# Weight slices converted in two pieces of 768 elements instead of three of 512

## The chip, the cores and the metric

The kernel runs on one core of a Trainium2 chip. The metric is the device time of one launch in microseconds (us). The kernel before was timed three times: 909.64, 910.88 and 911.83 us, median 910.88 us. The execution that was profiled took 909.49 us.

## The reference

Talking-heads attention is followed by a gated feed-forward layer. All inputs are 64-bit floats; the output is 32-bit.

```
scores = scale * q @ k^T                      # 4 batches, 12 heads, 448 x 448, depth 64
scores = einsum('bhij,hg->bgij', scores, w_pre)
attn   = exp(scores - max) / (sum + 1e-9)     # softmax over j
attn   = einsum('bhij,hg->bgij', attn, w_post)
x      = (attn @ v) as 1792 tokens x 768
h      = x @ w_in                             # 768 -> 2048
out    = (h * sigmoid(1.702 h)) @ w_out       # 2048 -> 768
```

## The kernel before

Attention runs in 180 softmax steps of ten query rows by twelve heads (45 a batch). A step is: gather of 120 score rows from DRAM (`r`, L295), mixing product on TensorE (`mx`, L312), maximum on VectorE (`nm`, L322), exponential on ScalarE (`e`, L332), sum on GpSimd (`rs`, L343), reciprocal on VectorE (L348), weighting on GpSimd (`wr`, L353), second mixing product on TensorE (`pp`, L363), and a copy out by ScalarE (`p`, L419). Batches 0 and 1 work in 32 bits, batches 2 and 3 in pairs of 16-bit numbers. Score products (`qk`, L247) run ahead of the steps. Every twelve steps make a chunk, and when its last copy is done, two context products (`av`, L441) multiply it with v. They share one PSUM bank. Their results become x, which the feed-forward layer reads.

The feed-forward layer (`h`, L604, and `po`, L642) takes the weights in 16 slices: `w_in` and `w_out` in eight each. [...] So `conversion` (L500 to L583) rebuilds 32-bit floats from the two 32-bit halves and then splits them into an upper and a lower 16-bit part. A slice goes through this in NP pieces of HW = WN // NP elements. For each piece there is a fetch on SyncE's queue (`w`, L513), `magnitude` on ScalarE (L520), `least`, `shift`, `rest` and `sign` on VectorE (L524, L528, L534, L540; each reads what the one before wrote) and `size`, a sum of squares on ScalarE with a read of its accumulator (L99). Once all pieces have a size, one small product on TensorE adds them over the partitions (L111, on `w_m`), VectorE makes a scale of it, and each piece gets `w_upper` on ScalarE (L568) and `w_lower` on VectorE (L573). The slice is then stored to DRAM (L579) and read back from there for each unit of the feed-forward layer (L592). Conversions run from 28 us (first fetch) to about 407 us (last store).

The sums of squares for v (`squares`, L134, which also calls L99) have the same form: a small product L111 on `mv`, whose result VectorE turns into a scale that the context's copies need.

The order of the work is not written out by hand. Each operation is entered with `add`: engines, a duration estimate (`occ`), dependences, a due time and, for a transfer, its size in MB. A planner (`run_all`) keeps a clock per engine and a model of the DMA queue. At each turn it takes the operation that can start first, the earlier due one where several can, and emits it. All instructions are in order on their engine, so the estimates set the order everywhere, also that of instructions that have nothing to do with the weights. Buffers are planned by tag: `w64` is the 64-bit staging, `wf` the 32-bit pieces, `wc` the 16-bit result.

Of the kernel before, what the change touches and what calls it, by code (L numbers as in the profile page):

```python
# [11 lines left out]
BF16 = mybir.dt.bfloat16  # L12
# [7 lines left out]
B, H, S, D = 4, 12, 448, 64  # L20
# [19 lines left out]
def attention_then_feed_forward(ctx, tc, q, k, v, w_pre, w_post, w_in, w_out, out):  # L40
# [6 lines left out]
    keep, stat, flow = pool("keep"), pool("stat", 4), pool("flow")  # L47
# [42 lines left out]
    def square_sum(x, m, eng):  # L90

        n = 1
        for d in x.shape[1:]:
            n *= d
        waste = flow.tile([128, 512], BF16, name="waste", tag="waste" + eng)[:x.shape[0], :n]
        if len(x.shape) == 3:
            waste = waste.rearrange("p (a b) -> p a b", b=x.shape[2])
        if eng == "A":
            nc.scalar.activation(waste, x, AF.Square, accum_out=m)  # L99
        else:  # L100
            nc.vector.scalar_tensor_tensor(
                waste, x, 1.0, x, op0=ALU.mult, op1=ALU.mult, accum_out=m
            )
# [380 lines left out]
    def scale_x(b):  # L484
# [8 lines left out]

    wd = {(kind, s): dram.tile([128, 2, WN], F16, name=f"wd{kind}_{s}", tag=f"wd{kind}_{s}")
          for kind in range(2) for s in range(NS)}
    NP = 3
    HW = WN // NP
    WF = 5

    def conversion(kind, s):  # L500

# [296 lines left out]
    def gated_by(x):  # L798

        if not 0 < x <= N:  # L800
            return []
        if x not in gates:
            gates[x] = add("-", 0.0, lambda: None, expos_at(x - 1), x, 0.0)
        return [gates[x]]
# [250 lines left out]
    def conversion_tasks(kind, s, first):  # L1055

        c = conversion(kind, s)
        due, sizes, low, wfs, pair = first + 7, [], [], [], []
        for a in range(NP):
            w64, wf = [], []  # L1060
            wfs.append(wf)
            j = add("SP", 0.4, lambda a=a: c["fetch"](a), gated_by(first + 2 * a), first + 2 * a, size=0.524, takes=[("w64", w64)])
            for n, (name, occ) in enumerate((("magnitude", 0.62), ("least", 0.35), ("shift", 0.35), ("rest", 0.61), ("sign", 0.61))):
                j = add("D" if n else "A", occ, lambda a=a, name=name: c[name](a), [j], due, occ + 0.09, takes=[] if n else [("wf", wf)])
                w64.append(j)
                if n:
                    wf.append(j)
            sizes.append(add("A", 0.63, lambda a=a: c["size"](a), [j], due + 0.2, 0.73))
            wf.append(sizes[-1])
        k = sums(c["total"], c["parts"], sizes, due)  # L1070
        k = conv_scale[kind, s] = add("D", 1.0, c["scale_w"], [k], due, 1.1)
        for a in range(NP):
            u = add("A", 0.62, lambda a=a: c["w_upper"](a, "A"), [k] + low[:0] + ([ups[0]] if a else []), due + 0.5, 0.72,
                    takes=[] if a else [("wc", pair)])
            if not a:
                ups = [u]
            low.append(add("D", 0.66, lambda a=a: c["w_lower"](a), [u], due + 0.5, 0.75))
            wfs[a] += [u, low[a]]
            pair += [low[a]] + ([u] if a else [])
        j = conv_done[kind, s] = add("SP", 0.4, c["store"], low, due, size=0.786)  # L1080
        pair.append(j)
# [3 lines left out]
    for b in range(B):  # L1085
        for c in range(NCH):
# [3 lines left out]
            for pr in range(NPAIR):  # L1090
                x = base - (18 if c == NCH - 1 else 17) + 2 * pr if c else base - 11 + pr
                if b == 0 and c == 1:
                    x = pr
# [13 lines left out]
    for n in range(2 * NS):  # L1107
        x = 7 * n if n <= NS else 7 * NS + 5 * (n - NS)
# [4 lines left out]
    for i in range(N):  # L1113
        if i + AHEAD < N:
            b, g = steps[i + AHEAD]
            n = i + AHEAD
            gathers[n] = add("SP", 0.4, lambda n=n: gather(n), sends.get((b, g // GPC), []), i,
                             size=0.215, takes=[("r", r_home[n])], behind=gathers.get(n - 1))
# [42 lines left out]
    for u in range(NU):  # L1161
        s, b = units[u]
        due = due_of["h", u, 0, 0]
# [5 lines left out]
        for fc in range(SF):  # L1169
            gen, th = [], []  # L1170
            j = None
# [87 lines left out]
```

## Time and profile before

| | before |
|---|---|
| timed runs, median (lowest to highest) | 910.88 us (909.64 to 911.83) |
| profiled execution | 909.49 us |
| its span on the core | 907.8 us |
| TensorE (PE) busy in the span | 878.1 us, 97% |
| VectorE (DVE) busy | 633.6 us, 70% |
| ScalarE (ACT) busy | 630.5 us, 69% |
| GpSimd (POOL) busy | 342.8 us, 38% |

The span runs from the first to the last instruction of the program; the execution has 1.69 us around it. In a view by windows the first two numbers of a row are the stretch and its length, then come the busy times of PE, of its weight loads (PEld), DVE, ACT and POOL with instruction counts, the granted TensorE clock (1.00 is full), the share of time that the DMA engines were busy, and GB/s. Length minus PE busy is PE's idle time in the stretch. In a view in order of time, the bracket at the end tells the idle time of the engine before the row and who ended it.

### The profile page before, as it was taken

What the parts mean: (1) busy time and instruction counts of PE and PEld (TensorE: products, weight loads), DVE (VectorE), ACT (ScalarE), POOL (GpSimd) and SP (SyncE); (2) the same over time, 40 slices, a digit from 0 to 9 for tenths busy, and PEclk for the clock granted to TensorE, in tenths of its full rate; (3) what the DMA queues carried; (4) which work ended last, traced back from release to release, by engine and by line L of the source; (5) the groups of instructions that cost most, each with busy time, mean ns of one, the idle gap of its engine ahead of it and who ended that gap; (6) DMA issues with size and microseconds to landing.
All of it is one profiled execution on the core that took longest, in us unless ns stands there. A gap on an engine that the chain in (4) does not pass through costs nothing.

```text
span 907.8 us, 19395 instructions
## 1 busy us (share of the span) xinstructions
PE 878.1 (97%) x7062; PEld 538.5 (59%) x7062; DVE 633.6 (70%) x1471; ACT 630.5 (69%) x1391; POOL 342.8 (38%) x538
## 2 busy tenths in 40 slices
PE   7889999999999999999999999999999999999998
PEld 5465666666566566655666656665656666545554
DVE  3668887678789988999678876679676664342233
ACT  2778888698877877876788797676776765323442
POOL 0212222222124221566346745547254663203332
PEclk9989999999999999999999999999999999999999
DMA  7878999998997796688587486568553432243422
GB/s 237 277 285 290 304 326 319 323 308 268 336 331 251 238 300 198 219 234 311 169 265 251 147 258 175 175 180 243 163 154 127 152 97 91 109 139 121 139 74 92
DMA packets 66402, 196.85 MB, mean 217 GB/s; under 512 B 7714, under 2 KB 32546, under 8 KB 66306
## 3 DMA queue, kind: packets, MB, share of 16 engines
q1 hardware_dynamic: 66306, 195.62, 66.7%
q8 instruction: 55, 0.90, 0.4%
q14 instruction: 41, 0.34, 0.1%
HBM read 138.96 MB, written 56.62 MB: 215 GB/s over the span
## 4 chain that ended last, share of the span: by engine, by line
PE 66%; DVE 13%; DMA 7%; ACT 7%; POOL 3%; issue 2%; SPq 1%; ACTq 0%; POOLq 0%; DVEq 0%
PE h L604 19%; PE po L642 18%; PE mx L312 5%; PE pp L363 5%; PE qk L247 3%; PE av L441 3%; PE av L452 3%; DMA vb<-in_v_dram 2%; PE qk L257 2%; DMA sd<-sc 2%; DVE nm L322 2%; DMA r<-sd 2%; PE mx L315 2%; PE pp L400 1%; PE pp L402 1%
## 5 line engine op out<-in xcount | busy, mean ns | idle before, releaser
L604 PE MATMUL h<-x,wt 128*128 128x448 f16 x1152 | 246.5, 352 | 2.0 <-DVE sc L273 0.9
L642 PE MATMUL po<-g,wt 128*128 128x448 f16 x1152 | 239.0, 352 | 2.4 <-DVE th L623 2.1
L604 PEld LDWEIGHTS <-wt 128*128 128x128 f16 x1152 | 108.9, 98 | 105.6 <-issue 15.6
L642 PEld LDWEIGHTS <-wt 128*128 128x128 f16 x1152 | 110.2, 98 | 101.5 <-issue 8.0
L343 POOL TENSOR_SCALAR rs<-sm 120x1 f32<-120x1 f32 x180 | 45.2, 251 | 319.0 <-ACT e L332 311.0
L322 DVE TENSOR_REDUCE nm<-mx 120x1 f32<-120x448 f32 x180 | 111.0, 617 | 36.4 <-PE mx L317 17.9
L670 POOL TENSOR_TENSOR acc<-acc,pt 128x448 f32<-128x448 f32 x69 | 78.7, 1141 | 114.0 <-ACT pt L664 113.3
L363 PEld LDWEIGHTS pp<-wr,e 120*112 120x112 f32 x720 | 85.1, 177 | 37.5 <-issue 18.7
L387 POOL TENSOR_TENSOR a<-w,a 120x448 f16<-120x448 f32 (+1 forms) x90 | 96.0, 1066 | 22.7 <-POOL w L373 11.2
L623 DVE SCALAR_TENSOR_TENSOR th<-th,h 128x448 f32<-128x448 f32 x64 | 39.5, 618 | 92.4 <-ACT th L619 92.1
L363 PE MATMUL pp<-wr,e 120*112 120x120 f32 x720 | 90.9, 270 | 3.9 <-POOL wr L353 3.7
L312 PE MATMUL mx<-r,wa 120*120 120x448 f32 x180 | 87.1, 569 | 5.8 <-DMA r<-sd 4.4
L332 ACT ACTIVATE e<-mx,nm,c 120x448 f32<-120x448 f32 (+1 forms) x90 | 65.3, 725 | 33.2 <-DVE nm L324 23.3
L373 POOL TENSOR_SCALAR w<-e,rs 120x448 f32<-120x448 f32 (+1 forms) x90 | 64.9, 721 | 42.7 <-DVE rs L348 25.1
L666 DVE SCALAR_TENSOR_TENSOR acc<-po,ct,acc 128x448 f32<-128x448 f32 x99 | 66.8, 677 | 15.9 <-PE po L642 15.3
L332 ACT ACTIVATE e<-mx,nm 120x448 f32<-120x448 f32 (+1 forms) x90 | 56.8, 632 | 28.5 <-DVE nm L322 24.9
L664 ACT ACTIVATE pt<-po,ct 128x448 f32<-128x448 f32 x69 | 43.6, 633 | 46.6 <-PE po L642 46.6
L381 ACT ACTIVATE a<-e,rs 120x448 f16<-120x448 f32 (+1 forms) x90 | 59.8, 668 | 20.2 <-DVE rs L348 17.4
L427 DVE TENSOR_TENSOR p<-pp,p 112x480 f16<-112x480 f32 (+1 forms) x90 | 58.3, 649 | 10.8 <-ACT p L423 10.1
L619 ACT ACTIVATE th<-h,ct 128x448 f32<-128x448 f32 x64 | 40.3, 630 | 36.0 <-PE h L604 36.0
L273 DVE SCALAR_TENSOR_TENSOR sc<-qk,sc 120x448 f16<-120x448 f32 (+1 forms) x96 | 55.5, 615 | 10.5 <-ACT sc L269 9.7
L423 ACT CAST p<-pp 112x480 f16<-112x480 f32 (+1 forms) x90 | 50.2, 557 | 17.8 <-PE pp L402 17.6
(141 smaller groups left out, 1604.7 us busy)
## 6 DMA issues: line engine op xcount, KB each, us to landing
wt<-wd SPq DMA_DIRECT2D x64, 768.0 KB
r<-sd SPq DMA_DIRECT2D x176, 210.0 KB
sd<-sc SPq DMA_DIRECT2D x66, 420.0 KB
w<-in_moe_w_in_dram SPq DMA_DIRECT2D x24, 512.0 KB
w<-in_moe_w_out_dram SPq DMA_DIRECT2D x24, 512.0 KB
wd<-w_p SPq DMA_DIRECT2D x16, 768.0 KB
sd<-sc SPq DMA_DIRECT2D x24, 308.0 KB
out_dram<-acc SPq DMA_DIRECT2D x24, 224.0 KB
```

Source lines behind the costliest of these rows:

```text
L312: nc.tensor.matmul(mx[:K, :S], st["wa"][:K, :K], r[:K, :], start=True, stop=True)
L322: nc.vector.tensor_reduce(nm[:K], row["mx", i][:K, :S], axis=AX.X, op=ALU.max, negate=True)
L332: nc.scalar.activation(e[:K], row.pop(("mx", i))[:K, :S], AF.Exp, bias=row.pop(("nm", i))[:K, 0:1], scale=1.0 if b < WHOLE else st["c", b] ...
L363: nc.tensor.matmul(pp[:CP, jc * K:(jc + 1) * K], e[:K, jc * CP:(jc + 1) * CP], wr[:K, :, :n], start=True, stop=True,)
L373: nc.gpsimd.tensor_scalar(w[:K], e[:K], row["rs", i][:K, 0:1], 1.0, op0=ALU.mult, op1=ALU.mult)
L381: nc.scalar.activation(a1[:K], row["e", i][:K], AF.Copy, scale=row["rs", i][:K, 0:1])
L387: nc.gpsimd.tensor_tensor(a2[:K], row.pop(("w", i))[:K], row["a1", i][:K], op=ALU.subtract)
L427: nc.vector.tensor_tensor(p[:, 1], row.pop(("pp", i)), p[:, 0], op=ALU.subtract)
L604: nc.tensor.matmul(h, w[:, i, c, fc * 128:(fc + 1) * 128], x[:, j, c, :], start=(n == 0), stop=(n == len(terms) - 1),)
L642: nc.tensor.matmul(po, w[:, j, fc, e * 128:(e + 1) * 128], g[:, i, fc, :], start=(n == 0), stop=(n == len(terms) - 1),)
L666: nc.vector.scalar_tensor_tensor(a, po, c, a, op0=ALU.mult, op1=ALU.add)
L670: nc.gpsimd.tensor_tensor(a, a, st.pop(("pt", u, e)), op=ALU.add)
```

## The change

NP goes from 3 to 2, so a piece has 768 elements. `w64` has NP buffers as before (its size in bytes stays), `wf` has three buffers of 768 in place of five of 512, and the unused output of `square_sum` (`waste`) grows to 768 columns. The planner's estimates for the pieces are raised to suit, and so the planner also orders the rest anew. The number of products on TensorE is the same; each sum on `w_m` now has two columns.

```diff
@@ -92,7 +92,7 @@
         n = 1
         for d in x.shape[1:]:
             n *= d
-        waste = flow.tile([128, 512], BF16, name="waste", tag="waste" + eng)[:x.shape[0], :n]
+        waste = flow.tile([128, 768], BF16, name="waste", tag="waste" + eng)[:x.shape[0], :n]
         if len(x.shape) == 3:
             waste = waste.rearrange("p (a b) -> p a b", b=x.shape[2])
         if eng == "A":
@@ -493,9 +493,9 @@
 
     wd = {(kind, s): dram.tile([128, 2, WN], F16, name=f"wd{kind}_{s}", tag=f"wd{kind}_{s}")
           for kind in range(2) for s in range(NS)}
-    NP = 3
+    NP = 2
     HW = WN // NP
-    WF = 5
+    WF = 3
 
     def conversion(kind, s):
 
@@ -1059,22 +1059,22 @@
         for a in range(NP):
             w64, wf = [], []
             wfs.append(wf)
-            j = add("SP", 0.4, lambda a=a: c["fetch"](a), gated_by(first + 2 * a), first + 2 * a, size=0.524, takes=[("w64", w64)])
-            for n, (name, occ) in enumerate((("magnitude", 0.62), ("least", 0.35), ("shift", 0.35), ("rest", 0.61), ("sign", 0.61))):
+            j = add("SP", 0.4, lambda a=a: c["fetch"](a), gated_by(first + 2 * a), first + 2 * a, size=0.786, takes=[("w64", w64)])
+            for n, (name, occ) in enumerate((("magnitude", 0.83), ("least", 0.48), ("shift", 0.48), ("rest", 0.88), ("sign", 0.88))):
                 j = add("D" if n else "A", occ, lambda a=a, name=name: c[name](a), [j], due, occ + 0.09, takes=[] if n else [("wf", wf)])
                 w64.append(j)
                 if n:
                     wf.append(j)
-            sizes.append(add("A", 0.63, lambda a=a: c["size"](a), [j], due + 0.2, 0.73))
+            sizes.append(add("A", 0.85, lambda a=a: c["size"](a), [j], due + 0.2, 0.95))
             wf.append(sizes[-1])
         k = sums(c["total"], c["parts"], sizes, due)
         k = conv_scale[kind, s] = add("D", 1.0, c["scale_w"], [k], due, 1.1)
         for a in range(NP):
-            u = add("A", 0.62, lambda a=a: c["w_upper"](a, "A"), [k] + low[:0] + ([ups[0]] if a else []), due + 0.5, 0.72,
+            u = add("A", 0.84, lambda a=a: c["w_upper"](a, "A"), [k] + low[:0] + ([ups[0]] if a else []), due + 0.5, 0.94,
                     takes=[] if a else [("wc", pair)])
             if not a:
                 ups = [u]
-            low.append(add("D", 0.66, lambda a=a: c["w_lower"](a), [u], due + 0.5, 0.75))
+            low.append(add("D", 0.93, lambda a=a: c["w_lower"](a), [u], due + 0.5, 1.02))
             wfs[a] += [u, low[a]]
             pair += [low[a]] + ([u] if a else [])
         j = conv_done[kind, s] = add("SP", 0.4, c["store"], low, due, size=0.786)
```

The first place is VectorE around step 22, where the planner had put the third piece of slice w0_1 between the maximum of step 22 (`nm_22`) and its reciprocal (`rs_22`). Before:

```order
L322 TENSOR_REDUCE nm_22_1010<-mx_22_991 120x1
L524 TENSOR_SCALAR w0_1_f2_1005<-w0_1_f2_1005 128x512
L528 TENSOR_SCALAR w0_1_f2_1005<-w0_1_f2_1005 128x512
L183 TENSOR_REDUCE e_wm_88<-wall2_940 128x1
L186 TENSOR_SCALAR e_wm_88<-e_wm_88 128x1
L187 TENSOR_SCALAR e_wm_88<-e_wm_88 128x1
L191 RECIPROCAL s_wm_1036<-e_wm_88 128x1
L192 TENSOR_SCALAR s_wm_1036<-s_wm_1036 128x1
L193 TENSOR_SCALAR wm1_86<-w_mix_82,s_wm_1036 120x120
L194 SCALAR_TENSOR_TENSOR wm2_87<-w_mix_82,s_wm_1036,wm1_86 120x120
L534 SCALAR_TENSOR_TENSOR w0_1_f2_1005<-w0_1_64_2_895,w0_1_f2_1005 128x512
L348 RECIPROCAL rs_22_1044<-rs_22_1044 120x1
```

and now:

```order
L322 TENSOR_REDUCE nm_22_982<-mx_22_963 120x1
L183 TENSOR_REDUCE e_wm_88<-wall2_914 128x1
L186 TENSOR_SCALAR e_wm_88<-e_wm_88 128x1
L187 TENSOR_SCALAR e_wm_88<-e_wm_88 128x1
L191 RECIPROCAL s_wm_995<-e_wm_88 128x1
L192 TENSOR_SCALAR s_wm_995<-s_wm_995 128x1
L193 TENSOR_SCALAR wm1_86<-w_mix_82,s_wm_995 120x120
L194 SCALAR_TENSOR_TENSOR wm2_87<-w_mix_82,s_wm_995,wm1_86 120x120
L115 TENSOR_REDUCE w0_1_n_1019<-pp_20_975 128x1
L348 RECIPROCAL rs_22_1017<-rs_22_1017 120x1
```

Three conversion instructions are gone from between them; the sum for the slice (L115, on `w0_1_n`) has come in.

The second place is TensorE where chunk 3 of batch 0 ends: step 44 is its last step, and `av_0_3_0` its first context product. Before:

```order
L363 MATMUL pp_42_1843<-wr_42_1796,e_42_1779 112x120 x4
L247 MATMUL qk_1_1_2_0_1855<-kf1_1_1216,qf1_1_1221 120x448
L247 MATMUL qk_1_1_2_1_1856<-kf1_1_1216,qf1_1_1221 120x448
L363 MATMUL pp_43_1870<-wr_43_1840,e_43_1820 112x120 x4
L363 MATMUL pp_44_1887<-wr_44_1882,e_44_1859 112x96 x4
L441 MATMUL av_0_3_0_1904<-p_0_3_1624,vf0_0_367 64x88 x16
L441 MATMUL av_0_3_0_1904<-p_0_3_1624,vf1_0_412 64x88 x8
L312 MATMUL mx_45_1934<-r_45_1813,wa_206 120x448
```

and now:

```order
L312 MATMUL mx_45_1795<-r_45_1722,wa_206 120x448
L363 MATMUL pp_43_1802<-wr_43_1790,e_43_1766 112x120 x4
L247 MATMUL qk_1_1_2_0_1815<-kf1_1_1177,qf1_1_1182 120x448
L247 MATMUL qk_1_1_2_1_1816<-kf1_1_1177,qf1_1_1182 120x448
L312 MATMUL mx_46_1824<-r_46_1727,wa_206 120x448
L363 MATMUL pp_44_1836<-wr_44_1832,e_44_1798 112x96 x4
L247 MATMUL qk_1_1_3_0_1851<-kf1_1_1177,qf1_1_1182 120x448
L247 MATMUL qk_1_1_3_1_1852<-kf1_1_1177,qf1_1_1182 120x448
L312 MATMUL mx_47_1861<-r_47_1747,wa_206 120x448
L363 MATMUL pp_45_1872<-wr_45_1859,e_45_1841 112x120 x4
L441 MATMUL av_0_3_0_1880<-p_0_3_1577,vf0_0_356 64x88 x16
L441 MATMUL av_0_3_0_1880<-p_0_3_1577,vf1_0_406 64x88 x8
```

Between `pp_44` and `av_0_3_0`, which follow each other directly before, there are now four rows: two halves of a score product, `mx_47` and `pp_45`.

The third place is TensorE at the end of the first chunk, with the sum for v (L111, on `mv_0`). Before:

```order
L363 MATMUL pp_10_601<-wr_10_596,e_10_575 112x120 x4
L111 MATMUL pp_10_601<-mv_0_470,ones_77 128x6
L363 MATMUL pp_11_629<-wr_11_619,e_11_606 112x120 x4
L441 MATMUL av_0_0_0_658<-p_0_0_290,vf0_0_367 64x120 x16
L441 MATMUL av_0_0_0_658<-p_0_0_290,vf1_0_412 64x120 x8
```

and now:

```order
L363 MATMUL pp_10_588<-wr_10_585,e_10_561 112x120 x4
L363 MATMUL pp_11_604<-wr_11_598,e_11_582 112x120 x4
L111 MATMUL pp_11_604<-mv_0_454,ones_77 128x6
L441 MATMUL av_0_0_0_637<-p_0_0_290,vf0_0_356 64x120 x16
L441 MATMUL av_0_0_0_637<-p_0_0_290,vf1_0_406 64x120 x8
```

The sum for v has moved behind `pp_11`. Such moves go on in the first half of the program; behind the first context products of batch 2 (`av_2_0_0`), TensorE's order is the same as before. On SyncE's queue the first gathers and fetches keep their order: r_4, piece 0 of w0_0, r_5, piece 1, a score store, r_6.

## Rows read from the trace of the kernel before

**Rows 1.** Page, busy time of the engines (us, share, instructions).

```profile
PE 878.1 (97%) x7062; PEld 538.5 (59%) x7062; DVE 633.6 (70%) x1471; ACT 630.5 (69%) x1391; POOL 342.8 (38%) x538
```

**Rows 2.** Windows by stage, columns as told under the table above.

```profile
25.00:58.15 33.15, 28.29 (x148) 15.86 (x146) 22.91 (x60) 28.79 (x72) 6.91 (x21) 0.98 0.93 311
58.15:75.00 16.85, 14.83 (x129) 11.10 (x130) 11.03 (x27) 10.46 (x27) 1.82 (x6) 0.84 0.56 181
75.00:173.00 98.00, 93.02 (x721) 61.58 (x720) 75.88 (x190) 81.35 (x200) 25.38 (x68) 1.00 0.97 323
173.00:250.00 77.00, 77.00 (x493) 47.56 (x492) 62.02 (x162) 66.44 (x163) 16.29 (x41) 1.00 0.94 304
250.00:430.00 180.00, 174.20 (x1298) 107.44 (x1298) 166.33 (x373) 137.47 (x309) 70.07 (x104) 1.00 0.81 260
430.00:907.80 477.80, 471.38 (x4193) 282.67 (x4191) 287.15 (x640) 299.50 (x613) 220.92 (x289) 1.00 0.50 158
```

**Rows 3.** Waits of PE: line, what ended them, us in total, times, longest.

```profile
PE mx L312 <- DMA r<-sd: 4.4, 5, 2.6
PE pp L363 <- POOL wr L353: 3.7, 6, 1.4
```

**Rows 4.** Conversion lines, 512 elements each: duration ns min/median/max, first and last start.

```profile
L520 ACT ACTIVATE w_f<-w x48: 650/671/707, 32.1 to 382.2; 128x512 f32<-128x512 f32 x48
L524 DVE TENSOR_SCALAR w_f<-w_f x48: 406/419/990, 32.8 to 388.8; 128x512 f32<-128x512 f32 x48
L534 DVE SCALAR_TENSOR_TENSOR w_f<-w,w_f x48: 673/692/1622, 34.6 to 394.4; 128x512 int32<-128x512 int32 x48
L540 DVE SCALAR_TENSOR_TENSOR w_f<-w,w_f x48: 673/689/1650, 35.3 to 397.9; 128x512 int32<-128x512 int32 x48
L99 ACT ACTIVATE waste<-w_f x48: 612/630/661, 37.5 to 399.3; 128x512 bf16<-128x512 f32 x48
L99 ACT ACTIVATION_READ_ACCUMULATOR waste<-w_f x48: 185/187/223, 38.0 to 399.8; 128x1 f32 x48
L568 ACT ACTIVATE w_p<-w_f,w_s x48: 705/718/743, 48.9 to 405.2; 128x512 f16<-128x512 f32 x48
L573 DVE SCALAR_TENSOR_TENSOR w_p<-w_f,w_s,w_p x48: 732/746/1525, 49.6 to 406.4; 128x512 f16<-128x512 f32 x48
```

**Rows 5.** Nearest other sizes, same columns; L353 is the softmax weighting on POOL.

```profile
L84 DVE TENSOR_SCALAR w_n<-w_n x16: 133/146/154, 46.8 to 402.5; 128x1 f32<-128x1 f32 x16
L222 DVE SCALAR_TENSOR_TENSOR kp<-kb,s_k,kp x6: 1140/1145/1379, 277.7 to 496.1; 128x896 f16<-128x896 f32 x6
L99 ACT ACTIVATE waste<-ka x12: 562/577/593, 232.7 to 469.4; 128x448 bf16<-128x448 f32 x12
L353 POOL TENSOR_SCALAR wr<-wp,rs x90: 358/366/803, 24.1 to 355.7; 120x120 f32<-120x120 f32 x88, 96x120 f32<-96x120 f32 x2
```

**Rows 6.** PE in order of time: start, us, instruction, [idle before <-releaser].

```profile
36.65 1.01 PE L312 MATMUL mx<-r,wa 120*120 120x448 f32 x2 [1.02 <-DMA r<-sd]
55.82 0.39 PE L111 MATMUL pp<-mv,ones 112*128 112x6 f32 x2 [1.43 <-ACT waste L99]
58.15 2.07 PE L441 MATMUL av<-p,vf 112*64 112x120 f32 x18 [0.66 <-ACT p L419]
...
93.79 1.07 PE L363 MATMUL pp<-wr,e 120*112 120x120 f32 x8 [1.43 <-POOL wr L353]
...
159.58 2.04 PE L441 MATMUL av<-p,vf 112*64 112x88 f32 x48 [1.94 <-ACT p L419]
```

**Rows 7.** DVE in order of time around 92 us, same columns.

```profile
90.08 0.43 DVE L528 TENSOR_SCALAR w_f<-w_f 128x512 int32<-128x512 int32 x1
...
92.09 0.69 DVE L534 SCALAR_TENSOR_TENSOR w_f<-w,w_f 128x512 int32<-128x512 int32 x1
92.70 0.16 DVE L348 RECIPROCAL rs<-rs 120x1 f32<-120x1 f32 x1
```

**Rows 8.** Window of the second fall of the granted clock, columns as in rows 2.

```profile
56.59:63.42 6.83, 5.97 (x54) 5.31 (x52) 4.60 (x14) 3.56 (x10) 0.00 (x0) 0.50 0.90 344
```

## The prediction

> **What bounds the kernel now.** I read the page's busy times first, then windows by stage, then PE's own waits, and last the stretches in which PE waits. The page shows PE busy for 878.1 us of a span of 907.8 us [rows 1]. The change leaves PE's products as they are, so it can only work on the 29.7 us in which PE is idle, and on the clock. The windows say where these lie: 4.9 us between 25 and 58 us, 2.0 up to 75, 5.0 up to 173, none from there to 250 (the feed-forward products then fill every hole), 5.8 from 250 to 430, and 6.4 behind that [rows 2]; the rest, 5.6, is the start before the first fetch. The order of PE is the same again soon after 430 us, and the conversions are over, so I leave the last stretch and the start as they are. What can move is 4.9 + 2.0 + 5.0 + 5.8 = 17.7 us. The other engines matter only where they end one of these waits. From 250 to 430 us VectorE is the tightest of them, 166.3 of 180 us busy; ScalarE has 137.5 [rows 2].
>
> **The change part by part.** *Fewer, longer instructions.* Each of the 16 slices loses five VectorE instructions (L524, L528, L534, L540, L573), three on ScalarE (L520, L99, L568), one accumulator read and one fetch. No instruction of 768 elements is in the trace, so I bound it. If time went wholly by elements, 768 would take 1.5 times 512 and nothing were saved. The nearest wider row is L222 with 896 elements, median 1145 ns [rows 5]; against L573 with 512, 746 ns [rows 4], that is 1.04 ns an element, and 768 would take 1012 ns. I take this slope for the three-operand lines. L573 then goes from 3 x 746 = 2238 to 2 x 1012 = 2024 ns, a saving of 214; L534 from 3 x 692 to 2 x 958, 160; L540 (689) 157. L524 stands at 419 ns, and a one-element instruction of its kind at 146 [rows 4, 5], which gives 0.53 ns an element, 555 ns at 768 and a saving of 147; L528 is of the same kind, another 147. VectorE saves 0.83 us a slice, 13.2 us in all, between 0 and that. On ScalarE, L99 takes 577 ns at 448 and 630 at 512 [rows 4, 5], 0.83 ns an element, so 212 more for 768: L520 saves 247, L568 294, L99 206 and one read 187, in all 0.93 us a slice, 14.9 us. Nearly all of this lies beside PE's work; it counts only at the places below.
>
> [...]
>
> *The end of the first chunk, 54 to 58 us.* PE waits 1.43 us before the sum for v, for ScalarE's squares, and 0.66 us before the first context product, for ScalarE's copies [rows 6]. In the new order `pp_11` stands ahead of that sum, which covers some of the first wait, but the context product still waits for the same copies behind the squares. What is gained is what ScalarE has less to do up to there: slice w0_0 whole (0.93) less the longer first piece of w1_0 (0.21), 0.72 us. I take -0.7; the ends are 0 and -2.1 (both waits).
>
> *Step 22, 92 us.* PE waits 1.43 us at `pp_22` [rows 6] for `wr`, which waits for the reciprocal at 92.70. Ahead of that reciprocal VectorE ran L524, L528 and L534 of a third piece, 0.42 + 0.43 + 0.69 us [rows 4, 7], and this piece no longer exists; a sum of 0.15 us moves in. I take -1.3; the ends are 0 and -1.4. Next late is then nothing on VectorE, but `pp_23`, which has its own chain.
>
> *The end of batch 0, 158 us.* `av_0_3_0` waits 1.94 us for the copy of `pp_44` [rows 6]. In the new order a score product, `mx_47` and `pp_45` stand between them, each as long as the 1.0 us of an `mx` [rows 6], or nearly. Three such blocks cover 1.94 us. I take -1.9; the ends are 0 (if `mx_47` waits for its gather in turn) and -1.9.
>
> *The rest up to 430 us.* Six slices (18 of the 48 pieces) lie between 250 and 430 us, so VectorE has 6 x 0.83 = 5.0 us less in a stretch in which it is idle for 13.7 us and PE for 5.8 [rows 2]. If VectorE were the sole cause, PE would gain 5.0; if each wait has its own chain, nothing. I take -1.5, nearer to nothing, because the waits are short and several end at ScalarE or at a transfer.
>
> *Larger fetches.* A piece of 128 x 768 numbers of 8 bytes is 768 KB instead of 512 KB. In the first microseconds r_5 stands behind one piece and r_6 behind two. At 311 GB/s [rows 2] 256 KB more take 0.84 us, so the gathers come 0.8 and 1.7 us later. PE waits there for gathers already: the longest after the start is 1.02 us at 36.65 [rows 6], of 4.4 us in all [rows 3]. Cover is thin, since no feed-forward product exists yet. I take +0.8; the ends are 0 and +1.7. Past 45 us PE does not wait for gathers, and there are 16 fetches less on SyncE's queue, which I count as nothing.
>
> *Waits that the new order makes.* The planner deals out the first half anew; some places will have less ahead of a wait than before. I take +1.0, two waits of 0.5 us, the size of the smaller ones; the ends are 0 and +5, a doubling of one stretch's idle time (75 to 173 us).
>
> The sum is -0.7 - 1.3 - 1.9 - 1.5 + 0.8 + 1.0 = -3.6 us. The profiled execution took 909.49 us, so 905.9; the median of the runs is 1.39 us above the profiled one, so 907.3 us.
>
> *The clock.* [...] The fall follows the idle stretch at 54 to 58 us. As that gets only 0.7 us shorter, I expect the fall to stay, at 0, with ends of -3.0 (it goes) and +3.0 (a second one comes).
>
> **The rivals.** *The gaps are dealt anew, and nothing is won.* The waits on the way of a softmax step are set by a planner whose estimates differ from the chip's by tenths of a microsecond; another order has another set of about 18 us of gaps. For it: the waits are many and short, and each has another releaser. Against it: three of the largest have a named cause that the change takes away. It gives the time of before, 910.9 us.
>
> [...]
>
> *Slower: the larger pieces ahead of the first gathers.* Its place is 28 to 58 us. r_5 and r_6 come 0.8 and 1.7 us later, `pp_5` stands behind them with nothing to cover, and the softmax chain carries the delay on into the first chunk's end, where a longer idle stretch brings a second fall of the clock. Price: +1.7, +3.0 for the clock, and +1.0 of new waits, against half of the 5.4 us of gains: +3.0, 912.5 us profiled, 913.9 as a median. For it: PE's waits for gathers in this stretch and a DMA share of 0.93 [rows 2]. Against it: the first slice's data is the same in total, and later gathers stand behind no more than before. It decides once the delays exceed the gains by 1.8 us.
>
> *The conversion gets no cheaper* (768 elements take 1.5 times 512): then the terms of ScalarE and of the rest fall away, -1.3 - 1.9 + 0.8 + 1.0 = -1.4, 909.5 us, inside the first rival's band.
>
> **How the numbers follow.** A measurement of this kernel can tell about 0.2%, 1.8 us, so "same" is 909.1 to 912.7 us. The forecast has 0.53, with its own range of 903.5 to 909. The gaps dealt anew, together with a conversion that gets no cheaper, have 0.27, and the larger pieces 0.20. The range is 902.5 to 913.5: below it lies only the case in which the clock's fall goes and the long stretch gains its 5.0 as well, and above it the worst of the slower case, together some 0.15. Faster 0.53, same 0.27, slower 0.20.
>
> **What would show it.** PE idle between 75 and 173 us falls from 5.0 to about 2; the bracket of 1.94 before an `av` near 158 us and that of 1.43 near 92 us are gone. VectorE's busy time falls by about 13 us, ScalarE's by up to 15. L534 stands near 958 ns and L524 near 555. The forecast is wrong if PE's idle time between 25 and 430 us stays at 17 us or more, and the slower rival is right if waits for `r` grow before 58 us and the clock is at 0.50 for more than one stretch behind 25 us.

## The result and the profile after

The kernel after takes 916.25 us (median of four runs, 915.99 to 917.81), the kernel before 910.26 us in the same comparison (909.51 to 911.83). The ratio is 1.0067 with a 95% interval of 1.0048 to 1.0086: slower by 0.7%, where 907.3 us was predicted. The profiled execution of after took 917.81 us, with a span of 916.1 us.

The page of after, busy time of the engines, answers to [rows 1]:

```profile
PE 880.4 (96%) x7062; PEld 539.5 (59%) x7062; DVE 622.4 (68%) x1392; ACT 622.9 (68%) x1327; POOL 346.8 (38%) x533
```

VectorE has 11.2 us less to do and ScalarE 7.6 us less. The conversion's own lines fell by more, on VectorE from 150.4 to 131.7 us and on ScalarE from 104.1 to 92.0; the rest of each engine's work changed too, because the planner may give a copy or an addition to either engine and dealt those anew as well. PE has the same 7062 products but 2.3 us more busy time. The span is 8.3 us longer: 2.3 us of PE's busy time and 6.0 us of idle time (29.7 before, 35.7 after).

The durations of the conversion lines in after (ns, min/median/max) answer to [rows 4]:

```profile
L520 ACT ACTIVATE w_f<-w x32: 881/912/946, 33.9 to 388.2; 128x768 f32<-128x768 f32 x32
L524 DVE TENSOR_SCALAR w_f<-w_f x32: 537/553/881, 34.8 to 391.9; 128x768 f32<-128x768 f32 x32
L534 DVE SCALAR_TENSOR_TENSOR w_f<-w,w_f x32: 939/957/1278, 36.7 to 394.4; 128x768 int32<-128x768 int32 x32
L540 DVE SCALAR_TENSOR_TENSOR w_f<-w,w_f x32: 937/953/1794, 37.8 to 395.8; 128x768 int32<-128x768 int32 x32
L573 DVE SCALAR_TENSOR_TENSOR w_p<-w_f,w_s,w_p x32: 1000/1012/1020, 49.7 to 410.3; 128x768 f16<-128x768 f32 x32
```

The forecast had 958 for L534, 555 for L524 and 1012 for L573. The instructions are not what went wrong, and the third rival, a conversion that gets no cheaper, falls. The windows of after, columns as in [rows 2], show where the time went:

```profile
25.00:58.15 33.15, 27.82 (x125) 14.56 (x124) 17.34 (x39) 23.04 (x54) 7.06 (x18) 0.85 0.88 300
58.15:75.00 16.85, 12.89 (x126) 9.74 (x125) 11.70 (x31) 11.47 (x27) 1.10 (x4) 0.90 0.52 172
75.00:173.00 98.00, 89.66 (x615) 57.99 (x615) 71.34 (x159) 76.70 (x175) 27.70 (x66) 0.97 0.89 291
173.00:250.00 77.00, 76.59 (x562) 48.43 (x559) 57.33 (x135) 61.82 (x144) 15.82 (x41) 1.00 0.93 310
250.00:430.00 180.00, 175.51 (x1306) 109.26 (x1304) 162.11 (x354) 137.92 (x294) 68.06 (x98) 1.00 0.82 262
```

PE's idle time is the length of a row less its first busy time. From 25 to 75 us it is 9.3 us (before: 6.9), from 75 to 250 us 8.7 (5.0), from 250 to 430 us 4.5 (5.8). Only the last of these gained. Together they rose by 4.9 us; the other 1.1 us of new idle time lie before 25 and behind 430 us. Next PE's waits in after (us in total, times, longest), which answer to [rows 3]:

```profile
PE pp L363 <- POOL wr L353: 8.0, 7, 3.1
PE mx L312 <- DMA r<-sd: 4.8, 3, 2.6
```

Waits for gathers took 0.4 us more than before; the waits for `wr` went from 3.7 to 8.0 us. The longest after the start, in order of time, against [rows 6]:

```profile
31.02 1.39 PE L312 MATMUL mx<-r,wa 120*120 120x448 f32 x2 [1.84 <-DMA r<-sd]
...
39.42 0.94 PE L363 MATMUL pp<-wr,e 120*112 120x120 f32 x3 [3.08 <-POOL wr L353]
...
99.33 1.55 PE L363 MATMUL pp<-wr,e 120*112 120x120 f32 x8 [2.17 <-POOL wr L353]
...
135.00 0.38 PE L111 MATMUL pp<-w_m,ones 128*128 128x2 f32 x2 [2.25 <-ACT waste L99]
...
137.35 1.94 PE L363 MATMUL pp<-wr,e 120*112 120x120 f32 x8 [1.01 <-POOL wr L353]
```

These are `mx_4`, `pp_5`, `pp_23` (the step behind the one whose wait of 1.43 us the change took away), the sum for slice w0_2 and `pp_35`. The 1.94 us before `av_0_3_0` are gone. The wait of `mx_4` is for r_4, which stands ahead of the first piece of weights on SyncE's queue; `mx_5` and `mx_6`, whose gathers stand behind pieces, do not wait. Before, `mx_4` started at nearly the same time, and PE came there without a pause:

```profile
30.87 0.92 PE L312 MATMUL mx<-r,wa 120*120 120x448 f32 x2
```

From the start of `mx_5` to that of `pp_5` it is 5.5 us before (33.02 to 38.54) and 5.3 after (34.12 to 39.42). So the chain of that step is no longer than it was; PE has less to do beside it. Last, the stretches of after in which the granted clock is at its lower level, columns as in [rows 8]:

```profile
31.50:34.90 3.40, 3.40 (x7) 0.96 (x6) 0.89 (x3) 1.51 (x3) 0.47 (x2) 0.50 1.00 301
38.30:45.20 6.90, 5.78 (x16) 2.96 (x18) 3.63 (x6) 4.03 (x9) 1.06 (x1) 0.51 1.00 308
62.20:65.60 3.40, 3.40 (x40) 3.36 (x36) 3.30 (x5) 1.01 (x3) 0.00 (x0) 0.51 0.61 214
99.80:103.20 3.40, 3.40 (x18) 2.10 (x19) 1.67 (x4) 0.61 (x2) 0.00 (x0) 0.50 0.97 338
137.30:140.70 3.40, 3.35 (x11) 2.51 (x12) 2.35 (x3) 2.45 (x5) 0.00 (x0) 0.50 0.06 21
```

Five stretches, 20.5 us in all, against two with 10.2 us before. Each follows a wait of PE: 1.84 us at 29.2, 3.08 at 36.3, 1.94 in two pieces around 60, 2.17 at 97.2 and 2.25 at 132.8 us. Not every wait is followed by a fall: the 1.94 us before `av_0_3_0` in before were not.

### The profile page after: what moved, and what is told of

Read it like the earlier page. It is cut to its first block, busy times and chain, and to the rows that moved or that the text cites. A ratio compares the mean times of both kernels' runs of the same rounds, so it can differ in the third digit from the quotient of the medians.

```text
span 916.1 us, 19201 instructions
## 1 busy us (share of the span) xinstructions
PE 880.4 (96%) x7062; PEld 539.5 (59%) x7062; DVE 622.4 (68%) x1392; ACT 622.9 (68%) x1327; POOL 346.8 (38%) x533
## 4 chain that ended last, share of the span: by engine, by line
PE 74%; DMA 9%; DVE 8%; ACT 3%; POOL 2%; issue 2%; SPq 1%; ACTq 0%; DVEq 0%; POOLq 0%
PE po L642 20%; PE h L604 20%; PE pp L363 6%; PE mx L312 6%; PE qk L247 3%; PE av L441 3%; PE av L452 3%; PE qk L257 3%; DMA r<-sd 2%; PE mx L315 2%; PE pp L400 2%; PE pp L402 1%; PE pp L401 1%; PE mx L317 1%; PE mx L316 1%
## 5 line engine op out<-in xcount | busy, mean ns | idle before, releaser
L343 POOL TENSOR_SCALAR rs<-sm 120x1 f32<-120x1 f32 x180 | 52.8, 293 | 325.5 <-ACT e L332 320.6
L670 POOL TENSOR_TENSOR acc<-acc,pt 128x448 f32<-128x448 f32 x65 | 75.4, 1160 | 109.9 <-ACT pt L664 109.3
L363 PE MATMUL pp<-wr,e 120*112 120x120 f32 x720 | 92.8, 273 | 8.9 <-POOL wr L353 8.0
L312 PE MATMUL mx<-r,wa 120*120 120x448 f32 x180 | 89.4, 581 | 6.7 <-DMA r<-sd 4.8
L666 DVE SCALAR_TENSOR_TENSOR acc<-po,ct,acc 128x448 f32<-128x448 f32 x103 | 69.5, 677 | 16.5 <-PE po L642 16.1
L664 ACT ACTIVATE pt<-po,ct 128x448 f32<-128x448 f32 x65 | 41.2, 633 | 47.7 <-PE po L642 47.7
L353 POOL TENSOR_SCALAR wr<-wp,rs 120x120 f32<-120x120 f32 (+1 forms) x90 | 44.9, 499 | 52.7 <-DVE rs L348 43.7
```

Source lines behind the costliest of these rows:

```text
L312: nc.tensor.matmul(mx[:K, :S], st["wa"][:K, :K], r[:K, :], start=True, stop=True)
L363: nc.tensor.matmul(pp[:CP, jc * K:(jc + 1) * K], e[:K, jc * CP:(jc + 1) * CP], wr[:K, :, :n], start=True, stop=True,)
L666: nc.vector.scalar_tensor_tensor(a, po, c, a, op0=ALU.mult, op1=ALU.add)
L670: nc.gpsimd.tensor_tensor(a, a, st.pop(("pt", u, e)), op=ALU.add)
```

## Experiments

**Sizes and order taken apart.** The planner deals out the order from its estimates, so the change alters two things at once. To part them, the planner's order was written out as a list of operations with their engines and emitted as it stands. big_old and big_old02 have the order of before, small_new that of after (the list itself and the lines that name the operations are left out here):

```diff
-    run_all()
+    for text in zlib.decompress(base64.b64decode(ORDER)).decode().split():
+        key, e = text.split(":")
+        j = by_key[key]
+        j["f"](e) if len(j["eng"]) > 1 else j["f"]()
```

> Pieces of 768 as in the change, but every other instruction in the order that the kernel before has on each engine: the old order is written into the kernel as a list, each slice's two pieces take the places of the old second and third piece, and the fetches the places of the old first and second. Theory 'order' (the loss comes from the new order of the rest): 906 to 911 us, PE idle between 25 and 173 us at 12 us or less. Theory 'size' (the loss comes from longer instructions on the way of the softmax step and larger fetches ahead of the gathers): 914 to 918 us, PE idle there near 17 us.

> As the first kernel with pieces of 768 in the old order, but the two pieces take the places of the old first and third piece, so the work on a slice begins as early as before. 'Order': 906 to 912 us, if it was the later start that cost the first such kernel its time. 'Size': still above 914 us. A third theory, 'fit' (any order is good only for the sizes that it was planned with): also above 914 us, but with the waits at other places than in the changed kernel.

> Pieces of 512 as before, but every other instruction in the order that the planner made for pieces of 768; the three pieces of a slice stand at the places of the two, the second right behind the first. Theory 'order': 914 to 919 us (the new order is bad whatever the size). Theory 'size': 908 to 912 us.

Times in us, with the ratio to before and its interval:

| order of | 512 elements | 768 elements |
|---|---|---|
| before | 910.3 | 921.4, 1.0136 [1.0088, 1.0183] (places of old pieces 2 and 3); 920.8, 1.0092 [1.0061, 1.0123] (1 and 3) |
| after | 917.4, 1.0086 [1.0055, 1.0118] | 916.3, 1.0067 [1.0048, 1.0086] |

Small pieces in the new order lose as much as the change, and mostly at the same places. PE in order of time in small_new (the kernel's lines have numbers higher by two in this file and in the others with a list):

```profile
35.64 1.01 PE L314 MATMUL mx<-r,wa 120*120 120x448 f32 x2 [3.00 <-DMA r<-sd]
...
40.65 1.74 PE L365 MATMUL pp<-wr,e 120*112 120x120 f32 x7 [2.42 <-POOL wr L355]
...
101.49 1.74 PE L365 MATMUL pp<-wr,e 120*112 120x120 f32 x7 [2.08 <-POOL wr L355]
```

The first of these rows can't be compared with after, since two pieces of 512 stand ahead of r_5 on this queue. But the waits of after at 36 and 97 us, 3.08 and 2.17 us, are here with 2.42 and 2.08. So they come mostly with the order, not with the longer instruction. Large pieces in the old order are no better: 921 us, beyond both ranges expected of big_old. That would fit an order that is good only for the sizes it was dealt for, but this isn't shown: in the new order both sizes take the same time. Which part of the change makes the loss can't be read from such a table; the order has to be varied for itself.

**The gathers put first.** The slower rival said that the larger fetches delay the first gathers. In after_fetch `r_5` goes ahead of the first piece of weights on SyncE's queue, `r_6` and `r_7` ahead of the second:

```diff
-  r_4, w0_0 piece 0, r_5, w0_0 piece 1, store, r_6, store, r_7
+  r_4, r_5, w0_0 piece 0, store, r_6, store, r_7, w0_0 piece 1
```

(This and the next show the order of the list, not code.)

> The changed kernel's own order, except on SyncE's queue: gather r_5 goes ahead of the first weight piece and r_6 and r_7 ahead of the second. If the larger fetches ahead of the gathers carry the loss of the first microseconds: PE's wait of 1.84 us before mx_5 (at 29 us) is gone, the 3.08 us before pp_5 fall to about 2, and the time is 2 to 4 us under the changed kernel's 916.3. If the waits there belong to the chain from mx_5 to pp_5: the sum of the two stays within 1 us of 4.9, the time 915 to 917.

It took 923.39 us, 1.0116 [1.0082, 1.0150]: slower still, and neither of the two times expected. PE in after_fetch, and below it VectorE at step 5:

```profile
34.24 1.07 PE L365 MATMUL pp<-wr,e 120*112 120x120 f32 x8 [0.74 <-POOL wr L355]
40.22 1.94 PE L365 MATMUL pp<-wr,e 120*112 120x120 f32 x8 [4.91 <-POOL wr L355]
```

```profile
36.28 0.56 DVE L526 TENSOR_SCALAR w_f<-w_f 128x768 f32<-128x768 f32 x1 [2.63 <-ACT w_f L522]
36.75 0.62 DVE L324 TENSOR_REDUCE nm<-mx 120x1 f32<-120x448 f32 x1
```

The wait of 1.84 us is gone. The expectation calls it one for `r_5` before `mx_5`; it was one for `r_4`, which stands ahead of the first piece in both orders, so its going is not the work of the exchange. The wait for `pp_5` grew from 3.08 to 4.91 us. In VectorE's order the conversion's first instruction (L526) stands ahead of step 5's maximum (L324): it waits 2.63 us for ScalarE's L522 and starts at 36.28 us, and the maximum comes behind it, at 36.75. So the larger pieces ahead of the gathers are not what makes the loss, and to put the gathers first makes it larger; but the rival's place, the first microseconds, was right.

**Named waits mended.** after_mend is after_fetch with the score product and `mx_6` put ahead of `pp_5`, another score product ahead of w0_2's sum, and at step 23 a copy ahead of L573 (L575 there). before_mend does in before what the forecast expected the new order to do: the sum for v behind `pp_11`, and `mx_45` and `mx_46` ahead of `av_0_3_0`.

```diff
-  pp_10, sum mv_0, pp_11, av_0_0_0 ...  pp_44, av_0_3_0, mx_45, mx_46      (before_mend)
+  pp_10, pp_11, sum mv_0, av_0_0_0 ...  pp_44, mx_45, mx_46, av_0_3_0
```

> As the one before, and three more moves: on PE pp_5 goes behind the score product and mx_6; the sum for slice w0_2 goes behind a score product; on VectorE the copy from PSUM beside step 23 goes ahead of L573, so that wr_23 meets no instruction with two SBUF inputs. 'Order' says: each of these waits shrinks by what is put ahead of it (3.08 by 1.8 us, 2.25 by 0.9), and the time falls to 910 to 913 us. [...] 'Size': no more than 1 us in all, 915 to 917.

> The kernel before in its own order, sizes as before, with the two moves on PE that the prediction counted on: the sum for v goes behind pp_11, and the first context product of batch 0's last chunk behind mx_45 and mx_46. If the terms were right: the wait of 1.94 us at 158 us is gone and that of 1.43 us at 54 us falls by 0.9, and the time is 907 to 909 us. If such waits only move to the next instruction: 910 to 911.

after_mend took 924.21 us, 1.0133 [1.0097, 1.0169]; before_mend 910.05 us, 0.9985 [0.9961, 1.0009], no difference. The first missed all its expected times, the second came out as expected for waits that only move. PE in before_mend:

```profile
55.45 1.07 PE L365 MATMUL pp<-wr,e 120*112 120x120 f32 x8 [1.45 <-POOL wr L355]
...
58.02 2.29 PE L443 MATMUL av<-p,vf 112*64 112x120 f32 x26 [1.36 <-ACT p L421]
...
158.99 2.04 PE L443 MATMUL av<-p,vf 112*64 112x88 f32 x48 [0.42 <-ACT p L421]
162.14 1.05 PE L443 MATMUL av<-p,vf 112*64 112x88 f32 x22 [1.11 <-DVE x L477]
```

The 1.94 us became 0.42, and the next `av` waits 1.11; the 1.43 us before the sum became 1.45 before `pp_11`. A wait is taken away and stands at the next instruction: what PE waits for is a chain on other engines, and the exchange on PE doesn't shorten that. PE in after_mend shows the same:

```profile
43.08 1.84 PE L249 MATMUL qk<-kf,qf 64*120 64x448 f32 x2 [5.62 <-ACT sc L281]
...
139.73 0.38 PE L113 MATMUL pp<-w_m,ones 128*128 128x2 f32 x2 [1.33 <-ACT waste L101]
...
142.07 1.94 PE L365 MATMUL pp<-wr,e 120*112 120x120 f32 x8 [1.96 <-POOL wr L355]
```

The 2.25 us before w0_2's sum became 1.33, and the next `pp` went from 1.01 to 1.96. The score product that was to cover the wait of `pp_5` waits itself, 5.62 us, for ScalarE to copy the scores of an earlier one. The third move didn't do what it was for: `wr_23` lasts 1.45 us in place of 1.17, and PE's wait at step 23 is 2.44 us in place of 2.17. So this run says nothing on what a `wr` of 0.37 us at that place would be worth.

**Other deals of the order.** If the time hangs on the order, other orders of the same work must scatter. Five of the planner's estimates for a piece were scaled, by 3 to 15%. The operations stay the same. Only their order changes, and with it the engine of a few that may go to either ScalarE or VectorE (of 96 copies of scores, L279, VectorE gets 21 to 30).

```diff
-  (("magnitude", 0.83), ("least", 0.48), ("shift", 0.48), ("rest", 0.88), ("sign", 0.88))   (after)
+  (("magnitude", 0.90), ("least", 0.52), ("shift", 0.52), ("rest", 0.95), ("sign", 0.95))   (after_more)
```

> The kernel before with the planner's five estimates for the conversion raised by 4 per cent (0.64, 0.365, 0.365, 0.635, 0.635); sizes unchanged, so only the order changes. Theory 'order': the time scatters with any new order, so it lies more than 1.8 us from 910.3 us, probably above (911 to 917). Theory 'size': 909 to 912 us, since no instruction is longer.

> The changed kernel with the same five estimates raised by 4 per cent (0.86, 0.50, 0.50, 0.92, 0.92). Theory 'order': it lies more than 1.8 us from 916.3 us, on either side (908 to 918). Theory 'size': 914 to 918 us, as the changed kernel.

> The kernel before, with the same five estimates 3 to 4% lower (0.60, 0.335, 0.335, 0.585, 0.585): 512-element pieces, another deal of the order. Deal: anywhere between 909 and 917 us. Size: at or below 912.7 us, as the two deals of 512 known so far (910.3 and 912.7).

> The kernel after, with the planner told that the five conversion instructions take 4% less than in after (0.80, 0.46, 0.46, 0.84, 0.84); the instructions themselves are after's, only the order they are dealt in differs. If a lucky or unlucky deal of the order made the 6 us, this is one more deal, and the time lies anywhere between 909 and 917 us, with a mean over the deals of 768 (after 916.3, estimates +4% 911.9, this, and +8%) within 2 us of the mean over the deals of 512. If the larger piece itself costs time, whatever the order, this run lies at 912 us or more, and the deals of 768 lie at least 3 us above those of 512 on average. I hold the first with 0.55.

> The kernel before with the five estimates 8% higher (0.67, 0.38, 0.38, 0.66, 0.66), nearer to what the trace of before has (0.67, 0.42, 0.42, 0.69, 0.69). Deal: between 909 and 917 us. Size: at or below 912.7 us. If better estimates help, faster than before, 909 us or less.

> The kernel after with the five estimates 8% higher (0.90, 0.52, 0.52, 0.95, 0.95), near what the instructions take in the trace of after (0.89, 0.58, 0.56, 0.95, 0.97). Deal: between 909 and 917 us. Size: 912 us or more. If the planner's estimates being too low is what cost the time, this run is the fastest of the deals of 768, 911 us or less.

> A fifth deal for pieces of 512: the five estimates at 0.71, 0.405, 0.405, 0.70, 0.70, the medians of the trace of before or a little over. Size with two opposite effects: PE idle for 5.5 to 7 us from 250 to 430 us, the clock at 0.50 for 7 to 14 us, none of it near 130 us, time between 909 and 916. Mere draw: no such bands. Better estimates help: at or below 909.

> A fifth deal of the order for pieces of 768: the five estimates at 0.95, 0.55, 0.55, 1.00, 1.00. In the four deals of 768 known so far (medians 916.3, 911.9, 915.7, 907.5, mean 912.8) PE is idle for 4.5, 3.9, 2.2 and 1.9 us from 250 to 430 us and the clock is at 0.50 for 20.5, 20.5, 23.9 and 13.7 us; in the four of 512 (910.3, 912.7, 915.0, 915.1, mean 913.3) idle for 5.8, 6.6, 5.7 and 6.3 us there, at 0.50 for 10.2, 6.8, 10.2 and 13.7. Size with two opposite effects: here 1.5 to 5 us idle from 250 to 430, 13 to 24 us at 0.50, one of these near 130 us, and a time between 906 and 917. Mere draw: these figures lie as often in the band of the 512-element deals (5.5 to 7 idle, 7 to 14 at 0.50). Better estimates help: at or below 909.

> A sixth deal for 512: 0.57, 0.32, 0.32, 0.56, 0.56. Size with two opposite effects: idle 5.5 to 7 us from 250 to 430, at 0.50 for 7 to 14 us, time between 909 and 916. Mere draw: no such bands. Worse estimates harm: at or above 915.

> A sixth deal for 768: 0.76, 0.44, 0.44, 0.81, 0.81. Size with two opposite effects: idle 1.5 to 5 us from 250 to 430, at 0.50 for 13 to 24 us with one fall near 130 us, time between 906 and 917. Mere draw: no such bands. Worse estimates harm: at or above 915.

The table gives the estimate for "magnitude", the median, the ratio to before, PE's idle time in three stretches (windows of the profiled execution), the busy time of `rs` and `wr` on GpSimd together (L343 and L353), and PE's wait for `wr`; all in us.

| | estimate | median | ratio [95%] | 25–75 | 75–250 | 250–430 | rs + wr | waits for wr |
|---|---|---|---|---|---|---|---|---|
| before_least | 0.57 | 909.4 | 0.9980 [0.9959, 1.0001] | 7.0 | 5.1 | 5.8 | 92.0 | 3.9 |
| before_less | 0.60 | 915.0 | 1.0049 [1.0020, 1.0079] | 8.9 | 7.8 | 5.7 | 88.2 | 5.4 |
| before | 0.62 | 910.3 | 1 | 6.9 | 5.0 | 5.8 | 87.6 | 3.7 |
| before_est | 0.64 | 912.7 | 1.0024 [1.0005, 1.0042] | 10.3 | 5.7 | 6.6 | 88.5 | 5.4 |
| before_more | 0.67 | 915.1 | 1.0046 [1.0022, 1.0071] | 8.1 | 9.8 | 6.3 | 95.2 | 8.3 |
| before_much | 0.71 | 910.8 | 0.9988 [0.9963, 1.0012] | 7.1 | 5.4 | 4.0 | 92.3 | 7.7 |
| **mean, 512** | | **912.2** | | 8.0 | 6.5 | 5.7 | 90.6 | 5.7 |
| after_least | 0.76 | 918.1 | 1.0085 [1.0058, 1.0112] | 8.3 | 10.4 | 3.8 | 103.2 | 9.3 |
| after_less | 0.80 | 915.7 | 1.0041 [1.0012, 1.0069] | 8.9 | 9.1 | 2.2 | 101.4 | 8.2 |
| after | 0.83 | 916.3 | 1.0067 [1.0048, 1.0086] | 9.3 | 8.7 | 4.5 | 97.7 | 8.0 |
| after_est | 0.86 | 911.9 | 1.0011 [0.9991, 1.0031] | 8.1 | 7.0 | 3.9 | 92.6 | 10.4 |
| after_more | 0.90 | 907.5 | 0.9952 [0.9924, 0.9980] | 8.5 | 6.2 | 1.9 | 100.9 | 5.3 |
| after_much | 0.95 | 910.5 | 1.0005 [0.9975, 1.0035] | 8.1 | 7.5 | 3.0 | 98.2 | 6.6 |
| **mean, 768** | | **913.3** | | 8.5 | 8.2 | 3.2 | 99.0 | 8.0 |

The same work, in another order, takes from 907.5 to 918.1 us (768) and from 909.4 to 915.1 us (512). The standard deviations are 4.0 and 2.5 us, so the difference of the means is +1.1 us, with a 95% interval of about -3.2 to +5.4 (1.9 us standard error, ten degrees of freedom). The size of the piece has no effect on the time that six deals each can show; a gain of 3 us, nearly the forecast's, would still fit. Of the 6.0 us between before and after, 1.1 lie between the means, 1.9 in a deal of before that is better than its mean and 3.0 in a deal of after that is worse than its own. That better estimates make a better order isn't shown either: for 768 the deals with higher estimates are faster, for 512 they aren't. after_more is faster than before.

Two columns do differ with the size. From 250 to 430 us PE is idle for 2.5 us less on average (1.9 to 4.5 against 4.0 to 6.6; 95% interval of the difference 1.2 to 3.7). And `rs` and `wr` take 8.4 us longer on GpSimd (4.0 to 12.7). All of it lies before 410 us, while weights are converted: up to there the two take 73.5 us on average with 512 and 82.0 with 768 (before 70.8, after 79.8), behind it 17.1 and 17.0 (16.8 and 17.9). The lines of before and, below them, of after:

```profile
L343 POOL TENSOR_SCALAR rs<-sm 120x1 f32<-120x1 f32 x180 | 45.2, 251 | 319.0 <-ACT e L332 311.0 <-DVE rs L348 3.1 <-PE mx L317 1.5
L353 POOL TENSOR_SCALAR wr<-wp,rs 120x120 f32<-120x120 f32 (+1 forms) x90 | 42.4, 471 | 52.0 <-DVE rs L348 36.7 <-PE mx L312 6.6 <-PE pp L363 2.7
```

```profile
L343 POOL TENSOR_SCALAR rs<-sm 120x1 f32<-120x1 f32 x180 | 52.8, 293 | 325.5 <-ACT e L332 320.6 <-PE mx L317 1.5 <-PE qk L257 0.2
L353 POOL TENSOR_SCALAR wr<-wp,rs 120x120 f32<-120x120 f32 (+1 forms) x90 | 44.9, 499 | 52.7 <-DVE rs L348 43.7 <-PE mx L312 2.3 <-PE pp L363 2.1
```

PE's waits for `wr` are 2.2 us longer on average, and its idle time from 75 to 250 us 1.7 us longer; neither is clear of the scatter between deals. The lower clock, which was at 20.5 us in after, is no column that differs: after_more has 13.7 us of it and after_much 3.4, before_more 13.7. The expectations of the last four deals had taken it for one (13 to 24 us and a fall near 130 us in each deal of 768); after_much and after_least have no fall there. They had also put PE's idle time from 250 to 430 us at 5.5 to 7 us for 512, and before_much has 4.0.

**GpSimd held up by VectorE.** Where the last column comes from stands in after_least, in order of time (PE, VectorE and GpSimd around 160 us):

```profile
158.64 4.18 POOL L353 TENSOR_SCALAR wr<-wp,rs 120x120 f32<-120x120 f32 x1 [0.36 <-DVE rs L348]
...
158.91 0.94 DVE L534 SCALAR_TENSOR_TENSOR w_f<-w,w_f 128x768 int32<-128x768 int32 x1
...
159.78 1.01 DVE L573 SCALAR_TENSOR_TENSOR w_p<-w_f,w_s,w_p 128x768 f16<-128x768 f32 x1
...
160.71 0.95 DVE L540 SCALAR_TENSOR_TENSOR w_f<-w,w_f 128x768 int32<-128x768 int32 x1
...
161.57 1.01 DVE L573 SCALAR_TENSOR_TENSOR w_p<-w_f,w_s,w_p 128x768 f16<-128x768 f32 x1
...
162.88 1.37 PE L363 MATMUL pp<-wr,e 120*112 120x120 f32 x7 [2.97 <-POOL wr L353]
```

One `wr` (the median of this line is 0.37 us) lasts 4.18 us and ends at 162.82 us, 0.24 us behind the last of four VectorE instructions with two inputs in SBUF, and PE waits 2.97 us for it. Its record starts 0.27 us ahead of the first of the four. In after, 19 of the 21 records of `wr` over 0.5 us overlap such an instruction (L534, L540 or L573), and 6 of the 69 shorter ones; in before, 26 of 29 and 15 of 61. Why a GpSimd instruction lasts longer beside them no trace here shows. In after the hold-up is smaller, beside an L540 at 37.80 us:

```profile
37.11 0.58 POOL L343 TENSOR_SCALAR rs<-sm 120x1 f32<-120x1 f32 x1 [2.12 <-ACT e L332]
37.72 0.16 DVE L348 RECIPROCAL rs<-rs 120x1 f32<-120x1 f32 x1
37.80 0.94 DVE L540 SCALAR_TENSOR_TENSOR w_f<-w,w_f 128x768 int32<-128x768 int32 x1
38.05 1.31 POOL L353 TENSOR_SCALAR wr<-wp,rs 120x120 f32<-120x120 f32 x1 [0.36 <-DVE rs L348]
```

`rs` takes 0.58 us in place of a median of 0.19, `wr` 1.31 in place of 0.37: together 1.3 us more, on the chain for which PE waits 3.08 us. To see whether the hold-up costs time, L534 and L540 were issued in halves, in two orders:

```diff
-            nc.vector.scalar_tensor_tensor(f, t["w", a][:, :, 0], 29, f, ...)
+            for h in (slice(0, HW // 2), slice(HW // 2, HW)):
+                nc.vector.scalar_tensor_tensor(f[:, h], t["w", a][:, h, 0], 29, f[:, h], ...)
```

> The kernel after, in its own order, but VectorE's two instructions of a piece with two inputs in SBUF (L534, L540) are each issued as two of 384 elements (32 x 2 x 2 = 128 instructions in place of 64). In after one wr of GpSimd took 1.31 us beside an L540 and one 1.17 us beside an L573, where most take 0.37. If long VectorE instructions that hold GpSimd up are what cost PE its waits (3.08 us for wr at 36 us), the halves let GpSimd in between them: that wait becomes 2.5 us or less, the mean of L353 falls from 499 towards 470 ns, and the time to 914 or less. If they are a side effect, the added fixed cost (64 x 0.2 us = 13 us on VectorE, of which a little lies on the path) makes 916 to 920. I hold the second with 0.65.

> The same two lines split in the same way, in the order of after_more (907.5 us). Hold-up by long instructions: 907 or less, L353's mean from 504 towards 470 ns. Side effect: 908 to 912, with PE idle for 1 to 2 us more from 250 to 430 us, where VectorE is busiest.

after_split took 917.41 us, 1.0070 [1.0046, 1.0095]: as after, which is the time expected for a side effect. The halves cost VectorE 6.5 us (L534 and L540 are busy for 69.7 us in place of 63.2), not 13; the 0.2 us for each was the author's estimate. more_split took 904.74 us (903.14 to 907.57), 0.9924 [0.9902, 0.9945]: the fastest of all, 6.3 us under before (911.03 there), which is the time expected if the hold-up counts; but its interval overlaps that of after_more. The lines of `rs` and `wr` (busy, mean ns), first in after_more, then in more_split:

```profile
L343 POOL TENSOR_SCALAR rs<-sm 120x1 f32<-120x1 f32 x180 | 55.6, 309 | 301.0 <-ACT e L332 295.5 <-PE mx L317 1.5 <-PE qk L257 0.2
L353 POOL TENSOR_SCALAR wr<-wp,rs 120x120 f32<-120x120 f32 (+1 forms) x90 | 45.3, 504 | 50.8 <-DVE rs L348 35.6 <-PE pp L363 6.1 <-PE qk L247 3.6
```

```profile
L343 POOL TENSOR_SCALAR rs<-sm 120x1 f32<-120x1 f32 x180 | 50.4, 280 | 299.8 <-ACT e L332 294.3 <-PE mx L317 1.5 <-PE qk L257 0.2
L353 POOL TENSOR_SCALAR wr<-wp,rs 120x120 f32<-120x120 f32 (+1 forms) x90 | 43.6, 485 | 55.5 <-DVE rs L348 37.7 <-PE pp L363 5.0 <-PE qk L247 3.8
```

The two lines fall by 6.9 us (in after_split by 4.1) in the same order of work, so the length of the two VectorE instructions is a cause of the hold-up; it rests on one trace of each kernel. PE's waits for `wr` hardly do: 5.3 to 5.2 us, and 8.0 to 8.0 in after_split. The long single waits got shorter (3.08 to 2.57 us at 36 us), others came. That the hold-up alone costs time is not shown.

## Why the prediction was wrong

The step that failed is "waits that the new order makes", taken at +1.0 us with +5 as its end, together with the three places whose gain was counted in full. PE's idle time between 25 and 430 us was to fall from 17.7 and rose to 22.5 us. The waits that the forecast named lost 4.8 us, and 9.7 us came elsewhere, against the +1.0.

- *The end of the first chunk*, -0.7: the two waits of 2.09 us together became 0.54 and 1.40, -0.15. *Step 22*, -1.3: its wait went, and one step later a wait of 0.57 us became one of 2.17. *av_0_3_0*, -1.9: it went, but at w0_2's sum and behind it PE now waits 2.25 and 1.01 us. before_mend shows why such gains can't be added up: with the order mended by hand at two of these places, the waits move on and the time stays.
- *The rest up to 430 us*, -1.5: measured -1.3, and -2.5 on average over the deals. This term, a stretch in which VectorE is busy for 166 of 180 us, was right in sign and near in size. It is the only gain in PE's idle time that stands clear of the deals' scatter.
- *What the conversion saves.* VectorE's five lines save 13.6 us if each instruction counts with its median, and the forecast had 13.2. They save 18.7 in all, because the time above the medians is 2.6 us in place of 7.7. ScalarE's saved 12.1, under the 14.9 of the forecast.
- *Larger fetches*, +0.8: waits for gathers grew by 0.4 us. The long one, 1.84 us, is for r_4, ahead of the pieces; behind them, the waits of 0.3 and 1.0 us before `mx_5` and `mx_6` are gone. One trace each doesn't tell so little as 0.4: before_mend has before's order of these transfers, and its waits for gathers are 6.3 us in place of 4.4.
- *The clock*, 0 with ends of 3.0 for the fall of [rows 8] that goes or a second one that comes: no run shows a fall to cost 3.0 us. Measured were 20.5 us at the lower level, 0.50, in place of 10.2, and 2.3 us more busy time of PE for the same products. Each fall came behind a wait, so this term hangs on the first, but not by a fixed price: in big_old PE is idle for 11.2 us from 25 to 75 us at a granted clock of 1.00.
- *Waits for `wr`*, for which the sum has no term: they grew by 4.3 us in after and by 2.2 on average over the deals, which the scatter doesn't tell from 0. That `rs` and `wr` take longer is shown, 99.0 us on average in place of 90.6; that PE waits longer for them is not.

The first rival had the cause: the gaps are dealt anew. Its time was not that of before, though, since a deal is no zero but a draw: other orders of the same work lie 5 us above and 6 below their mean. The forecast gave such a draw the time of before, within the 1.8 us that a measurement can tell. What the change itself does to the time, +1.1 us with an interval of -3.2 to +5.4, is smaller than the draw, and its sign stays open. That after lies as high as it does is bad luck of the deal; with the estimates of after_more the same pieces are faster than before by 0.5%.

## What to carry to other kernels

Where a planner or a scheduler orders the work, a change of size also draws a new order. Before a gain or loss of under 1% is put down to the change, draw several orders of both versions (a few per cent on an estimate is enough) and compare the means and the columns by stage. Count a wait that is named in the profile as gained only if the chain that feeds it gets shorter, or if one engine is busy for nearly the whole stretch.

## What was not expected of the hardware

In after_least one GpSimd instruction, with a median of 0.37 us, lasted 4.18 us, beside four VectorE instructions of 0.94 to 1.01 us in a row. With pieces of 768 the 270 instructions of `rs` and `wr` took 99.0 us in all on average, with 512 they took 90.6. And the executions of one program mostly differ with the clock: in after_less ten runs went from 913.33 us at a mean granted clock of 0.991 to 919.29 at 0.981, though in before_est 909.50 us came at 0.994 and 914.78 at 0.996. So one profile of a kernel, such as that of after_much (904.94 us, with a median of 910.5), can be far from its median.
